# Pairing token tiles for seven block products from the third batch on

## The chip, the cores and the metric

The kernel runs on one core of one Trainium2 chip. The metric is the device time of one launch in microseconds (us). The engines named here are TensorE (PE, matmuls; PEld is its weight load), VectorE (DVE), ScalarE (ACT), GpSimd (POOL) and SyncE (SP), which issues DMAs.

## What is computed

Attention with RMS-normalised q and k (8 batches, 12 heads, 448 positions, head size 64), and behind it a feed-forward layer with a PReLU (768 to 2048 to 768) on the 3584 tokens:

```python
q_n, k_n = rmsnorm(q, g_q), rmsnorm(k, g_k)      # x / sqrt(mean(x*x) + 1e-6) * g
scores = np.matmul(q_n, k_n.transpose(0, 1, 3, 2)) / 8
attn = softmax(scores)                           # over the keys
x = np.matmul(attn, v)                           # heads side by side: (3584, 768)
h = x @ w_in                                     # (3584, 2048)
g = np.maximum(h, 0.0) + alpha * np.minimum(h, 0.0)
out = g @ w_out                                  # (3584, 768), float32
```

## The kernel before

**Groups and steps.** Four heads of a batch make a group y (three per batch, 24 in all). A group's scores are seven tiles of 128 keys by 2x448 queries. Lines 679 to 719 deal these 168 tiles out to 69 steps; the main loop (line 917) issues one step after the other, and since the schedule is manual, the order of the code is the order of every engine's queue. A step has two to four score tiles; some steps also have a softmax denominator (`dens`), a product with v (`avs`), the turn of a group's q and k, and then fillers (`gaps`) that keep TensorE at work. A pair of groups (y, y+1) has its denominator in one step and its product with v in the next (41 and 42, 57 and 58). The third group of a batch, from y = 8 on, has both in one step (28, 36, 44, 52, 60, 68).

**What a group needs.** `load_qk` brings q and k on SP (ring "nat"), `square` squares them on POOL (ring "sq"), `reduce` sums on DVE, `root` makes the inverse root on ACT (two operations on rr, lines 173 and 174), `scale` multiplies on POOL (ring "qs", line 179), `turn_dma` transposes by DMA on SP (rings qT, kT), and `turn` multiplies kT by the gains on DVE (line 288). `soft` (line 343) takes the exponential of a score tile on ACT. For the third group of a batch, `add_up` sums these exponentials over the tiles on POOL, six additions (line 356), and `den_pre` makes the denominator from that sum with matmuls "dnb" (line 389), which DVE copies (line 397); ACT then takes logarithm and exponential (lines 401 and 410), and DVE multiplies the product with v by it into xT (line 439).

**Fillers.** `up(b, ft)` makes one of 16 blocks of g for a batch: six matmuls (line 454), alpha times h on ACT into a tile "ah" (line 494), the maximum on DVE into gT (line 498). `down(b0, t, oh)` makes one half of the columns of one tile of 128 tokens: 16 matmuls (line 508), a copy on DVE (line 520), two DMAs. gT holds two batches, seven token tiles. Lines 773 to 850 deal the fillers out by a cost for each (`UP` 1.13, `DOWN` 2.6).

**Banks.** ups, downs, dnb and half of the products with v take turns on two PSUM banks (`psf`, tag "mm"). The next user of a bank waits until the last reader of it is done.

**Block products.** The last six token tiles (22 to 27) are done in pairs: `quad` computes two tiles times w_out, cut in 2x2 blocks, with seven block products of eight matmuls each in place of eight. It needs sums of blocks of g (`mix`, on POOL, lines 563 to 566) and differences of blocks of w_out (`mix_weights`, 16 operations on POOL at the end of step 60, line 554):

```python
nc.gpsimd.tensor_add(out=g[:, 0], in0=block(t + 1, 0), in1=block(t + 1, 1))
nc.gpsimd.tensor_sub(out=g[:, 1], in0=g[:, 0], in1=block(t, 0))
nc.gpsimd.tensor_sub(out=g[:, 2], in0=block(t, 0), in1=block(t + 1, 0))
nc.gpsimd.tensor_sub(out=g[:, 3], in0=block(t, 1), in1=g[:, 1])
```

After step 68 come one down, the 16 ups of the last batch, and the three quads.

Of the kernel before, what the change touches and what calls it, by code (L numbers as in the profile page):

```python
# [9 lines left out]
FP32 = mybir.dt.float32  # L10
# [11 lines left out]
def kernel(  # L22
# [72 lines left out]

    nat, sqs, qs, ss_t, rr_t, qkT, vt, xT = {}, {}, {}, {}, {}, {}, {}, {}
# [3 lines left out]
    def load_qk(y, hold=False):  # L100
        b, i = divmod(y, G)
        for nm in "qk":
            t = ld.tile([128, 2, J, D], FP32, name="nat", tag="nat", bufs=6)
            if hold and nm == "q":

                nc.scalar.copy(out=t[:, 0, 0, 0:1], in_=expb)
            for g in range(2):
                (nc.scalar if y < 2 and g else nc.sync).dma_start(
                    out=t[ds(64 * g, 64)].rearrange("p h j d -> p h (j d)"),
                    in_=SRC[nm][b, g, :, ds(2 * i, 2)],  # L110
                )
            nat[y, nm] = t

    def load_v(b):
        t = att.tile([128, HH, J, D], FP16, name="vt", tag="vt")
# [28 lines left out]
    def square(y, nm):  # L144
        src = nat[y, nm].rearrange("p h j d -> p (h j d)")
        sq = ld.tile([128, 2 * J, D], FP32, name="sq", tag="sq", bufs=4)
# [29 lines left out]
    def scale(y, nm):  # L176
        t = ld.tile([128, J, 2, D], FP16, name="qs", tag="qs", bufs=4)
# [11 lines left out]
    def part_square(nm, h, j, eng):  # L189
        if ("sq", nm) not in tops:  # L190
            tops["sq", nm] = ld.tile([128, 2 * J, D], FP32, name="sq", tag="sq", bufs=4)
# [24 lines left out]
    def part_scale(nm, j, n, eng):  # L216
        if (0, nm) not in qs:
            qs[0, nm] = ld.tile([128, J, 2, D], FP16, name="qs", tag="qs", bufs=4)
# [15 lines left out]
    def part_copy(nm, j, eng):  # L234
        if (0, nm) not in qkT:
            qkT[0, nm] = att.tile([128, J, 2, 64], FP16, name=f"{nm}T", tag=f"{nm}T", bufs=4)
# [17 lines left out]
    def turn_one(y, nm):  # L254
# [6 lines left out]
        t = att.tile([128, J, 2, 64], FP16, name=f"{nm}T", tag=f"{nm}T", bufs=4)  # L261
# [12 lines left out]
    def turn_dma(y):  # L274
        for nm in "qk":
            t = att.tile([128, J, 2, 64], FP16, name=f"{nm}T", tag=f"{nm}T", bufs=4)
# [7 lines left out]
    def turn(y):  # L284
# [20 lines left out]
        for tp, nm in zip(tps, "qk"):  # L305
            t = att.tile([128, J, 2, 64], FP16, name=f"{nm}T", tag=f"{nm}T", bufs=4)
# [166 lines left out]
    def up(b, ft, spare=False):  # L473
# [8 lines left out]
        ah = ffn.tile([128, S], FP16, name="ah", tag="ah", bufs=3)  # L482
        if b == 0 and ft in (2, 3, NF - 4):

            nc.vector.tensor_scalar(
                out=ah, in0=hT[:, :S], scalar1=alpha_sb[:, ft : ft + 1], scalar2=None,
                op0=ALU.mult,
            )
            if ft < 4:

                held.append((hT, ah, ft))
                return
        else:
            nc.scalar.activation(  # L494
                out=ah, in_=hT[:, :S], func=AF.Copy, scale=alpha_sb[:, ft : ft + 1]
            )
        for hT, ah, ft in [(hT, ah, ft)] + (held if b == 0 and ft == 4 else []):
            nc.vector.tensor_max(out=gT[:, ft, ds((b & 1) * S, S)], in0=hT[:, :S], in1=ah)  # L498

    def down(b0, t, oh, jobs=(), spare=False):  # L500

        op = bank("op", spare)
        parts = 2 if (b0, t, oh) == (B - 2, J - 1, 1) else 1
        PW = OH // parts
        ops = [op] + [bank("op", False) for _ in range(parts - 1)]
        for c in range(parts):
            for ft in range(NF):
                nc.tensor.matmul(  # L508
                    out=ops[c][:, :PW],
                    lhsT=gT[:, ft, ts(t, 128)],  # L510
                    rhs=w_out_sb[:, ft, ds(oh * OH + c * PW, PW)],
                    start=(ft == 0),
                    stop=(ft == NF - 1),
                )
# [3 lines left out]
        o = ffn.tile([128, OH], FP32, name="osb", tag="osb", bufs=4)  # L518
        for c in range(parts):
            nc.vector.tensor_copy(out=o[:, ts(c, PW)], in_=ops[c][:, :PW])  # L520
# [3 lines left out]
        last = (b0, t) == (B - 2, J - 1)  # L524
        for c in range(parts):
            for half in range(2):
                bb, j = divmod(2 * t + half, J)
                (nc.scalar if last and half else nc.sync).dma_start(
                    out=out4[b0 + bb, j, :, ds(oh * OH + c * PW, PW)],
                    in_=o[ds(64 * half, 64), ts(c, PW)],  # L530
                )

    HF = NF // 2
    QF = HF // 2
    tw, mixes = {}, {}

    def mix_weights():

        def w(f, m, p):
            return w_out_sb[:, ds(HF * f + QF * p, QF), ts(m, OH)]  # L540

        for p in range(2):
            for n in range(4):
                tag, bufs = ("nat", 6) if (p, n) not in ((1, 2), (1, 3)) else ("sq", 4)
                tw[n, p] = ld.tile([128, QF, OH], FP16, name="tw", tag=tag, bufs=bufs)
        for n, x, y in (
            (0, (0, 1), (0, 0)), (1, (1, 1), 0), (3, (1, 0), 1), (2, (1, 1), (0, 1))
        ):
            for p in range(2):
                a = w(*x, p)  # L550
                b = tw[y, p] if y in (0, 1) else w(*y, p)
                for c in range(2):
                    r = ts(c, QF // 2)
                    nc.gpsimd.tensor_sub(out=tw[n, p][:, r], in0=a[:, r], in1=b[:, r])

    def block(t, f):
        return gT[:, ts(f, HF), ts(t, 128)]

    def mix(t):

        g = att.tile([128, 4, HF, 128], FP16, name="gs", tag="expT", bufs=EB)
        mixes[t] = g
        nc.gpsimd.tensor_add(out=g[:, 0], in0=block(t + 1, 0), in1=block(t + 1, 1))  # L563
        nc.gpsimd.tensor_sub(out=g[:, 1], in0=g[:, 0], in1=block(t, 0))
        nc.gpsimd.tensor_sub(out=g[:, 2], in0=block(t, 0), in1=block(t + 1, 0))
        nc.gpsimd.tensor_sub(out=g[:, 3], in0=block(t, 1), in1=g[:, 1])

    def send(b0, t, oh, o, c=slice(0, None), split=False):
        for half in range(2):
            bb, j = divmod(2 * t + half, J)  # L570
            dst = out4[b0 + bb, j, :, ts(oh, OH)]
            (nc.scalar if split and half else nc.sync).dma_start(
                out=dst[:, c], in_=o[ds(64 * half, 64), c]
            )

    def quad(b0, t, wide, last=False):

        s1, s2, s3, s4 = (mixes[t][:, n] for n in range(4))
# [15 lines left out]

        def whole(f, m):
            return lambda ft: w_out_sb[:, HF * f + ft, ts(m, OH)]

        def mixed(n):
            return lambda ft: tw[n, ft // QF][:, ft % QF]

        def product(bank, g, v, first, c=slice(0, OH)):
            for ft in range(HF):
                nc.tensor.matmul(  # L603
                    out=bank[:, c], lhsT=g[:, ft], rhs=v(ft)[:, c],
                    start=(first and ft == 0), stop=(ft == HF - 1),
                    skip_group_check=True,
                )

        def part(name):
            return ld.tile([128, OH], FP32, name=name, tag="qs", bufs=4)  # L610

        def result():
            return ffn.tile([128, OH], FP32, name="osb", tag="osb", bufs=4)

        u = {}

        def m1():
            product(x, block(t, 0), whole(0, 0), True)
            u[1] = part("m1")
# [469 lines left out]
```

## Time and profile before

| what | us |
| --- | --- |
| median of 3 runs (423.75 to 424.4) | 424.37 |
| the profiled execution | 425.34 |
| its span, first to last instruction | 423.5 |
| ACT busy | 278.4 (66%) |
| steps 10 to 68 begin | 36.7 to 368.6 |
| ups and quads after step 68 end | 419.6 |

The mean granted TensorE clock is 0.992: it is 0.83 between 10 and 30 us, and 1.00 from 30 us on. A line of a group gives the source line, the engine and operation, what it writes and reads with the shape, the count, busy time and mean ns of one, and the engine's idle time just ahead of it with what ended it. A line of a timeline gives start, duration, engine, line, operation, and in brackets the idle time before it. The steps' starts are the starts of their first score tiles (line 329).

### The profile page before, as it was taken

The page shows a single profiled execution, that of the slowest core. Times are in us where ns is not written, and L with a number is a line of the kernel's source. Part 1 is how long each engine was busy: PE and PEld are TensorE (multiplying, and loading weights), DVE is VectorE, ACT ScalarE, POOL GpSimd, SP SyncE. Part 2 cuts the span into 40 slices and gives each one's busy share as a digit, 9 for nine tenths or more (in the row PEclk, how much of TensorE's full clock was granted, in tenths as well). Part 3 has the DMA queues.
Part 4 walks back from the last instruction along what each step waited for, and adds up shares of the span by engine and source line. Part 5 has one row for each costly group of instructions (what it writes and reads, how often), then busy time and mean ns, then how long its engine had stood idle before and what let it go on. Part 6 is the DMA issues. An engine that isn't in the chain of part 4 may idle for free.

```text
span 423.5 us, 11140 instructions
## 1 busy us (share of the span) xinstructions
PE 411.3 (97%) x4731; PEld 214.7 (51%) x4731; DVE 224.7 (53%) x335; ACT 278.4 (66%) x390; POOL 290.9 (69%) x201
## 2 busy tenths in 40 slices
PE   7899999999999999999999999999999999999996
PEld 3335445544455545554555545554555545555564
DVE  3866964556474545547465364646464253455322
ACT  5798888778856677667847578467865478155110
POOL 6689995384996479481993649753790999960870
PEclk9889999999999999999999999999999999999999
DMA  8999999999756974649255973548215500110144
GB/s 184 239 240 211 193 207 184 201 212 220 129 125 112 195 141 108 104 98 218 58 129 97 174 183 86 98 100 177 46 38 104 107 14 21 29 30 2 29 96 101
DMA packets 68530, 53.37 MB, mean 126 GB/s; under 512 B 35568, under 2 KB 68480, under 8 KB 68480
## 3 DMA queue, kind: packets, MB, share of 16 engines
q1 hardware_dynamic: 53520, 39.54, 43.4%
q0 software_dynamic: 13984, 11.81, 18.8%
q10 hardware_dynamic: 976, 1.31, 1.2%
q8 instruction: 37, 0.61, 0.6%
q14 instruction: 13, 0.11, 0.1%
HBM read 45.62 MB, written 11.01 MB: 134 GB/s over the span
## 4 chain that ended last, share of the span: by engine, by line
PE 85%; ACT 6%; DVE 4%; POOL 2%; DMA 1%; issue 1%; POOLq 0%; ACTq 0%
PE op L508 23%; PE hT L454 21%; PE sc L329 8%; PE hTa L454 8%; PE av L368 5%; PE opa L508 4%; ACT expT L343 3%; PE oq L603 3%; PE dn L368 3%; POOL rden L356 2%; PE avb L368 2%; PE oqm L603 2%; ACT ah L494 2%; PE dnb L389 2%; PE spin L671 1%; DVE gT L498 1%
## 5 line engine op out<-in xcount | busy, mean ns | idle before, releaser
L343 ACT ACTIVATE expT<-sc,expb 128x896 f16<-128x896 f32 x168 | 161.6, 1003 | 44.7 <-PE sc L329 44.4
L179 POOL TENSOR_TENSOR qs<-nat,rr 128x896 f16<-128x896 f32 x41 | 69.1, 1707 | 81.7 <-issue 39.3
L454 PE MATMUL hT<-xT,w_in_sb 128*128 128x448 f16 x558 | 115.7, 353 | 0.8 <-DVE gT L498 0.5
L454 PEld LDWEIGHTS <-w_in_sb 128*128 128x128 f16 x768 | 73.2, 98 | 74.0 <-issue 9.4
L508 PE MATMUL op<-w_out_sb,gT 128*128 128x384 f16 x592 | 101.4, 326 | 0.5 <-DVE gT L498 0.5
L508 PEld LDWEIGHTS <-gT 128*128 128x128 f16 x704 | 66.1, 98 | 53.0 <-issue 11.8
L494 ACT ACTIVATE ah<-hT,cols 128x448 f16<-128x448 f32 x92 | 58.1, 632 | 41.8 <-PE hT L454 40.9
L498 DVE TENSOR_TENSOR gT<-hT,ah 128x448 f16<-128x448 f32 x93 | 57.9, 623 | 48.8 <-ACT ah L494 48.0
L155 POOL TENSOR_TENSOR sq<-nat 128x896 f32<-128x896 f32 (+1 forms) x47 | 75.4, 1625 | 8.4 <-DMA nat<-in_q_dram 7.8
L356 POOL TENSOR_TENSOR rden<-rden,expT 128x896 f32<-128x896 f32 x30 | 56.8, 1895 | 2.4
L329 PE MATMUL sc<-qT,kT 64*32 64x448 f16 (+1 forms) x1092 | 54.9, 359 | 3.5 <-ACT expT L343 1.4
L163 DVE TENSOR_REDUCE ss<-sq 128x14 f32<-128x896 f32 (+1 forms) x48 | 48.8, 1038 | 2.5 <-POOL sq L155 2.5
L520 DVE COPY osb<-op 128x384 f32<-128x384 f32 x37 | 20.5, 556 | 53.0 <-PE op L508 52.5
L454 PE MATMUL hTa<-xT,w_in_sb 128*128 128x448 f16 x198 | 42.8, 352 | 0.0
L329 PEld LDWEIGHTS <-kT 64*32 64x32 f16 (+1 forms) x1092 | 16.6, 93 | 36.1 <-issue 29.8
L494 ACT ACTIVATE ah<-hTa,cols 128x448 f16<-128x448 f32 x33 | 20.9, 634 | 15.3 <-PE hTa L454 15.2
L498 DVE TENSOR_TENSOR gT<-hTa,ah 128x448 f16<-128x448 f32 x33 | 20.6, 624 | 17.6 <-ACT ah L494 17.0
L439 DVE TENSOR_TENSOR xT<-av,rden 128x896 f16<-128x896 f32 x16 | 17.5, 1091 | 21.5 <-ACT rden L410 15.5
L368 PEld LDWEIGHTS <-vt 64*32 64x32 f16 (+1 forms) x1260 | 21.7, 94 | 12.4 <-issue 2.5
L368 PE MATMUL av<-expT,vt 64*32 64x448 f16 (+1 forms) x812 | 26.3, 349 | 0.0
L508 PE MATMUL opa<-w_out_sb,gT 128*128 128x384 f16 x112 | 19.4, 327 | 0.0
L563 POOL TENSOR_TENSOR gs<-gT 128x1024 f16<-128x1024 f16 x3 | 6.4, 2122 | 16.7 <-DVE gT L498 16.7
(98 smaller groups left out, 331.9 us busy)
## 6 DMA issues: line engine op xcount, KB each, us to landing
nat<-in_q_dram SPq DMA_DIRECT2D x46, 224.0 KB, 4.4
nat<-in_k_dram SPq DMA_DIRECT2D x46, 224.0 KB, 4.7
out_dram<-osb SPq DMA_DIRECT2D x107, 96.0 KB, 2.2
vt<-in_v_dram POOLq DMA_DIRECT2D x16, 336.0 KB, 5.8
w_in_sb<-in_moe_w_in_dram POOLq DMA_DIRECT2D x12, 256.0 KB, 7.4
w_out_sb<-in_moe_w_out_dram POOLq DMA_DIRECT2D x4, 768.0 KB, 12.1
nat<-in_q_dram ACTq DMA_DIRECT2D x2, 224.0 KB, 4.6
nat<-in_k_dram ACTq DMA_DIRECT2D x2, 224.0 KB, 5.8
```

What stands on the lines that cost most here:

```text
L155: nc.gpsimd.tensor_mul(out=sqf[:, c], in0=src[:, c], in1=src[:, c])
L163: nc.vector.tensor_reduce(out=o[:, c], in_=sqs[y, nm][:, c], axis=AXIS_X, op=ALU.add)
L179: eng.tensor_mul(out=t.rearrange("p j h d -> p h j d"), in0=nat[y, nm], in1=rr_t[y][:, "qk".index(nm)].unsqueeze(3).broadcast_to((128, 2, ...
L329: nc.tensor.matmul(out=sc[ds(64 * g + m * c, m), par, :S].rearrange("p (j c) -> p j c", j=J), lhsT=kT[ds(64 * par, 64), j, g, ts(c, m)], r ...
L343: nc.scalar.activation(out=expT[y][:, j], in_=scs[y, j][:, :, :S], func=AF.Exp, scale=QK_SCALE, bias=expb[:, 0:1],)
L356: nc.gpsimd.tensor_add(out=s, in0=e[:, 0] if j == 1 else s, in1=e[:, j])
L368: nc.tensor.matmul(out=accs[g][ds(m * h, m), :S], lhsT=weights(g, y, par, ts(c, m), j), rhs=expT[y][ds(64 * g, 64), j, par, :], start=(j = ...
L454: nc.tensor.matmul(out=hT[:, :S], lhsT=w_in_sb[:, g * G + i, ts(ft, 128)], rhs=xT[b][:, g, i, :], start=(i == 0 and g == 0), stop=(i == G ...
L494: nc.scalar.activation(out=ah, in_=hT[:, :S], func=AF.Copy, scale=alpha_sb[:, ft : ft + 1])
L498: nc.vector.tensor_max(out=gT[:, ft, ds((b & 1) * S, S)], in0=hT[:, :S], in1=ah)
L508: nc.tensor.matmul(out=ops[c][:, :PW], lhsT=gT[:, ft, ts(t, 128)], rhs=w_out_sb[:, ft, ds(oh * OH + c * PW, PW)], start=(ft == 0), stop=(f ...
L603: nc.tensor.matmul(out=bank[:, c], lhsT=g[:, ft], rhs=v(ft)[:, c], start=(first and ft == 0), stop=(ft == HF - 1), skip_group_check=True,)
```

## The change

**Pairs from the third batch on.** Tiles 0 to 7 stay downs; tiles 8 to 21 become seven more pairs. A pair's work is cut in three fillers: `quad_a` (three products, 24 matmuls), `quad_b` and `quad_c` (two products each). Each keeps a PSUM bank over two products and adds on DVE. A table written by hand replaces the dealing-out from step 28 on.

```diff
+    def quad_a(tile, jobs=()):
+        s2 = mixes[tile][1]
+        x, y = (psf.tile([128, 512], FP32, name="qx", tag="mm") for _ in range(2))
+        product(x, block(tile, 0), w_block(0, 0), True)
+        u2 = result()
+        nc.vector.tensor_copy(out=u2, in_=x[:, :OH])
+        some(jobs)
+        product(y, s2, tw[1], True)
+        nc.vector.tensor_add(out=u2, in0=y[:, :OH], in1=u2)
+        some(jobs)
+        product(x, block(tile, 1), w_block(1, 0), False)
+        o = result()
+        nc.vector.tensor_copy(out=o, in_=x[:, :OH])
+        send(tile, 0, o)
...
+    def quad_b(tile, jobs=(), late=False):
...
+        product(z, s3, tw[2], True)
+        u3 = result()
+        nc.vector.tensor_add(out=u3, in0=z[:, :OH], in1=u2)
+        some(jobs)
+        product(p, s1, tw[0], True)
+        nc.vector.tensor_add(out=u3, in0=p[:, :OH], in1=u3)
+        send(tile + 1, 1, u3)
...
+    def quad_c(tile, jobs=()):
+        u2, z, p = kept[tile]
+        product(z, block(tile + 1, 1), tw[3], False)
+        o = result()
+        nc.vector.tensor_add(out=o, in0=z[:, :OH], in1=u2)
+        send(tile + 1, 0, o)
+        some(jobs)
+        product(p, mixes[tile][3], w_block(1, 1), False)
+        nc.vector.tensor_add(out=u2, in0=p[:, :OH], in1=u2)
+        send(tile, 1, u2)
...
+    table = (
+        "d d|u4|u4|u4|u4|d d|d|d d|"
+        "a8|b8 c8|u5|u5|u6|a10|b10|c10|"
+        "a12|u4|u4|u4|u4|b12 c12||a14|"
+        "b14 c14|u4|u4|u4|u4|a16|b16|c16|"
+        "a18|u4|u4|u4|u4|b18 c18|a20|b20|"
+    ).split("|")
...
+    rest = list(units("c20 u16"))
```

The table's first entry is step 28, so `a8` is step 36 and `b20` step 67. `some(jobs)` issues one waiting operation, a reduce or a turn of k. Batch 1's ups move a little (steps 21 to 24 get 5, 4, 4 and 3 of them, before 4, 4, 4 and 3), and step 25 gets two downs in place of a down and an up.

**Mixing.** The sums of a pair are made in two parts: s1 and s2 on DVE at the start of a step, s3 and s4 on POOL at the end of one, behind the additions of that step. s3 is written over gT itself. The 16 operations on w_out are spread over steps 17 to 28 and 35, and one of the four differences is written over w_out.

```diff
+    def mix_two(tile, eng, own=False):
...
+        eng.tensor_add(out=s1, in0=block(tile + 1, 0), in1=block(tile + 1, 1))
+        eng.tensor_sub(out=s2, in0=s1, in1=block(tile, 0))
+    def mix_rest(tile):
+        s1, s2, s3, s4 = mixes[tile]
+        nc.gpsimd.tensor_sub(out=s3, in0=block(tile, 0), in1=s3)
+        nc.gpsimd.tensor_sub(out=s4, in0=block(tile, 1), in1=s2)
...
+    for n, y in ((35, 8), (41, 10), (43, 12), (50, 14), (57, 16), (59, 18), (66, 20)):
+        at(n, mix_two, y, nc.vector)
+    for n, y in ((35, 8), (41, 10), (44, 12), (51, 14), (57, 16), (60, 18), (66, 20)):
+        after(n, mix_rest, y)
+    for k in range(3 * PIECES):
+        n, p = divmod(k, PIECES)
+        after(17 + k, mix_weights, (0, 1, 3)[n], p)
+    for p in range(PIECES):
+        after(35, mix_weights, 2, p)
```

**Room.** The mixed blocks stay in SBUF from step 17 on in an "arena" that early loads, squares and scaled tiles borrow first. To make room for it the rings get shorter: nat 6 to 4, sq 4 to 2, qs 4 to 2, qT and kT 4 to 3, v 2 to 1; osb gets 6 in place of 4. The tile ah goes: ACT writes alpha times h into gT and DVE takes the maximum there. From y = 11 on a load is issued behind the scale of the group two before it, and v's load behind the last product of the batch before.

```diff
+        low = y > 3 * G + 1
+        if low:
+            after(root_at[y - 2], load_qk, y)
...
-    for b in range(1, B):
-        at(av_at[G * b] - 6, load_v, b)
+    at(av_at[G] - 6, load_v, 1)
+    for b in range(2, B):
+        after(av_at[G * b - 1] + 1, load_v, b)
```

## The prediction

> **What bounds the kernel now.** I read the page's busy shares first, then the stretches of 10 us, then the groups, and last three timelines step by step.
>
> ```profile
> PE 411.3 (97%) x4731; PEld 214.7 (51%) x4731; DVE 224.7 (53%) x335; ACT 278.4 (66%) x390; POOL 290.9 (69%) x201
> PEclk9889999999999999999999999999999999999999
> L508 PE MATMUL op<-w_out_sb,gT 128*128 128x384 f16 x592 | 101.4, 326 | 0.5 <-DVE gT L498 0.5
> L356 POOL TENSOR_TENSOR rden<-rden,expT 128x896 f32<-128x896 f32 x30 | 56.8, 1895 | 2.4
> ```
>
> TensorE sets the time: 97% busy, and in the stretches from 180 us on it is busy 9.6 to 10 us of every 10. So each matmul removed is time gained, as long as TensorE finds no wait in its place. A mean share hides where that can happen, so I looked at the stage with the least room. POOL, then TensorE, from step 56 to step 60:
>
> ```profile
> 298.56 3.33 POOL L179 TENSOR_TENSOR qs<-nat,rr 128x896 f16<-128x896 f32 x2 [8.50 <-issue]
> 301.86 3.32 POOL L155 TENSOR_TENSOR sq<-nat 128x896 f32<-128x896 f32 x2
> 305.13 1.88 POOL L356 TENSOR_TENSOR rden<-expT 128x896 f32<-128x896 f16 x1
> 307.09 9.80 POOL L356 TENSOR_TENSOR rden<-rden,expT 128x896 f32<-128x896 f32 x5
> ```
>
> ```profile
> 296.33 0.57 PE L329 MATMUL sc<-qT,kT 64*32 64x448 f16 x16
> ...
> 312.00 2.77 PE L508 MATMUL opa<-w_out_sb,gT 128*128 128x384 f16 x16
> 314.71 0.57 PE L329 MATMUL sc<-qT,kT 64*32 64x448 f16 x16
> 315.21 5.37 PE L508 MATMUL op<-w_out_sb,gT 128*128 128x384 f16 x32
> 320.52 0.57 PE L329 MATMUL sc<-qT,kT 64*32 64x448 f16 x16
> 320.90 1.28 PE L389 MATMUL dnb<-rden,ones 64*32 64x448 f32 x12
> ```
>
> Step 56 starts at 296.33. POOL idles until the step's root is there (ScalarE's second rr ends at 298.43), then works without a gap: two scales, two squares, six adds, to 316.89. The denominator matmul dnb, which needs the sixth add, starts at 320.90. **So POOL has 4.0 us of room in this stage, and no more**; it hangs on the start of step 56, so it can't work ahead. In step 28 the room is 0.2 us (adds end 124.38, dnb 124.57). Third, DVE around dnb in step 44:
>
> ```profile
> 220.30 1.91 DVE L288 TENSOR_SCALAR kT<-kT,gain 128x896 f16<-128x896 f16 x1
> ...
> 224.16 1.16 DVE L397 COPY rden<-dnb 128x448 f32<-128x448 f32 x2 [1.18 <-PE dnb L389]
> 227.38 1.09 DVE L439 TENSOR_TENSOR xT<-av,rden 128x896 f16<-128x896 f32 x1 [2.06 <-ACT rden L410]
> 228.39 2.07 DVE L163 TENSOR_REDUCE ss<-sq 128x14 f32<-128x896 f32 x2
> 230.37 1.25 DVE L520 COPY osb<-op 128x384 f32<-128x384 f32 x2
> ```
>
> DVE stands still for 2.06 us for ScalarE's logarithm and exponential; what is queued behind xT waits too. Today that is a copy nobody needs soon.
>
> **What goes.** Seven more pairs (tiles 8 to 21), each of 56 matmuls of 384 columns in place of 64, so 56 matmuls in all. A group of 16 takes 2.60 us between starts (315.21 to 320.52 holds 32 and two score tiles), 162.5 ns each: 56 x 162.5 ns = **9.1 us** less. The last three pairs stay. Moved at no cost: the 16 tw pieces leave the end, and with them most of the wait before dnb in step 68 (368.4 to 369.4, worth 1.0 us). The ah tile goes; ScalarE writes gT itself, after matmuls that the new table finishes steps earlier. Shorter nat, qs, q/k and v rings: each load or turn comes 4 to 7 steps (some 24 us) after the one whose buffer it takes and lands in 3 to 6 us; sends wait on SP behind the same scales as now. I cost these at nothing; were a load late once per batch it would be 1 to 2 us each.
>
> **What comes, by stage.** Natural arrival is what TensorE would reach without new waits. An up unit is 1.14 us, a down 2.6, the thirds of a pair a, b, c 3.9, 2.6, 2.6.
>
> Steps 17 to 28 (T1). Nine tw pieces (1.65 us each, the L554 rows) enter POOL ahead of the sixth add of y 8: 14.9 us. One fits a wait for a load (82.4 to 85.3). The other eight, 13.2 us, have the 5.6 us idle before 106.06 and 1.1 us more because step 24 begins one up later; 6.5 are left. TensorE comes 2.6 us later (a down more, the same ups), less the 1.1 us already counted, and 0.2 was free, so dnb waits **4.8 us**. If only the two pieces behind step 24's scales counted, it would be 3.3 - 1.5 - 0.2 = 1.6.
>
> Steps 40 to 44 (T3). mix_rest adds two POOL operations of 2.12 us (the gs rows) before adds four to six: 4.25. TensorE's own work shrinks from 17.2 to 15.9 (six ups, a, b, c). Room 4.0: 4.25 + 1.3 - 4.0 = 1.5 us. Then the k-turn of step 43 stands on DVE between c's two evictions. Turns took 0.44 us with POOL idle and up to 1.91 (the row above) with POOL busy, ending 0.25 us after POOL's operation. So c's last eviction ends some 0.9 us after the sixth add, and dnb needs that bank: **2.5 us**.
>
> Steps 56 to 60 (T6). The same, with more TensorE work gone: 17.2 to 13.65 (four ups, a, b, c). 4.25 + 3.6 - 4.0 = 3.8, and 0.8 for the turn: **4.6 us**, half at b (it needs s3), half at dnb.
>
> Steps 48 to 52 (T5). No mix before the adds, but step 50 has no filler, a's first bank waits for the xT products, behind the mixing on DVE, and the turn sits between a's evictions: dnb 2.7 us late; c's first product 0.8, its second 0.3: **3.8 us** (0.5 if DVE is free).
>
> Steps 36 and 44 (T2, T4). Quad a follows dnb. Its third product accumulates into the bank that DVE must copy first, and that copy is behind xT (ends 5.76 us after dnb starts; product three could start 5.5 after): 0.85 us. The last copy is behind two reduces of 1.07, and the next unit takes that bank: 1.4 us. **2.2 + 2.25 us.** Step 60 has no reduces (T7): **1.15**.
>
> Steps 66 and 67 (T8). b of tile 20 needs s3, behind three adds: 2.45 us late; less the 1.0 us that goes: **1.45**.
>
> mix_two on DVE (two operations, 1024 f16 columns, both inputs in SBUF) has no row. Below: the turn's 0.44 for 896. Above: 1.23 each, from DVE's L179 of 1.09 for 896, plus up to 1.9 of waiting if POOL is at work. I take 1.23 without the wait, since that row is the nearest with two SBUF inputs. With a wait each time on the path T3, T5 and T6 grow by about 2 us each, +6.
>
> Sum: -9.1 + 4.8 + 2.2 + 2.5 + 2.25 + 3.8 + 4.6 + 1.15 + 1.45 = **+13.65 us**. The profiled execution took 425.34 (span 423.5): 439.0. It stands 1.0 above the median of the runs, 424.37; on that basis 438.0.
>
> One rule speaks on that last doubt. The trace's row: POOL's scale at 30.36 took 2.51 us instead of 1.69, beside DVE's two-input L179 (30.23 to 31.32); the reverse order isn't shown. The Trainium skill, page "SBUF — State Buffer", section "SBUF: two separate sides", says DVE and GpSimd hold a shared port pair as an exclusive lock, also when DVE reads two SBUF inputs. By the page mix_two would wait for POOL's operation each time, and the sum would be about +20.
>
> **Rivals.** (1) Only POOL's sums bind; evictions and banks are hidden: 4.8 + 1.5 + 0.5 + 3.8 + 1.45 - 9.1 = +2.95, 427.3. For it: idle time on DVE is half the span. Against: the order on DVE is fixed. (2) Every mix_two waits for POOL: 13.65 + 6, 444.0. For it: the turn rows. (3) The other side: POOL's chain is not tied to the step, so the scales of steps 24, 40, 48 and 56 start when POOL is free. For it: 8.50 us idle there, which the profile books as "issue". Against: the scales start 0.13 us after rr. If they start 4 us earlier everywhere, dnb finds its adds ready, T1, T3, T5, T6 and T8 fall to about 1.5 together, and 1.5 + 5.6 - 9.1 = -2.0: 422.4; with DVE hidden too, 415.3. It decides once all new waits are under 9.1 us. (4) That fewer matmuls aren't issued can be left out: the loops count them.
>
> **Numbers.** Forecast 0.62 (432 to 443), rival 1 0.18, rival 2 0.07, rival 3 0.11, within 0.2% 0.02 (0.2%, 0.85 us, is what a measurement can tell from no change). Faster 0.11, same 0.02, slower 0.87. The range leaves out rival 3 and the far end of rival 2: 426 to 447.
>
> **What would show it.** TensorE's busy share falls to about 92% (411.3 - 9.1 over 437.2); dnb waits on POOL's rden in steps 28, 44 and 60 and on DVE's evictions; the third product of a waits on DVE after xT in steps 36, 44, 60; b of tiles 16 and 20 wait on POOL's s3. I am wrong if dnb of step 28 waits less than 2 us, if scales start well before their step's rr, or if TensorE stays over 96% busy.

## The result and the profile after

The changed kernel takes **453.69 us** (median of 4 runs, 452.13 to 456.44) against 424.38 (4 runs beside it): a ratio of 1.0695, 95% interval 1.0634 to 1.0756. That is 29.3 us slower. The forecast was 13.65 slower and the range ended at 447.0. The profiled execution took 454.77 us, its span is 453.0 and its mean granted clock 0.970. From here on, lines are those of the changed kernel: score 356, exponential 370, up 481, alpha on ACT 521, maximum 525, down 543, square 178, reduce 186, scale 206, turn of k 315, additions 383, dnb 416, xT 464 and 466, operations on w_out 574, the two sums on VectorE (mix_two) 589 and 590, the two on POOL (mix_rest) 595 and 596, products 600, evictions of a 619 to 626, of b 640 and 643, of c 654 and 658.

The page first, the four rows that were read of before:

```profile
PE 414.4 (91%) x4675; PEld 212.5 (47%) x4675; DVE 268.5 (59%) x370; ACT 278.6 (61%) x390; POOL 323.8 (71%) x215
PEclk9999999996999999989998999899899899999999
L383 POOL TENSOR_TENSOR rden<-rden,expT 128x896 f32<-128x896 f32 x30 | 59.4, 1979 | 3.4 <-ACT expT L370 1.4
L543 PE MATMUL op<-w_out_sb,gT 128*128 128x384 f16 x208 | 35.4, 326 | 0.0
```

TensorE issues 56 matmuls fewer and is yet busy 3 us longer, over a span 29.5 us longer. Busy time that grows while work falls is a slower clock: the PEclk row has a 6 and several 8s from 100 us on, where before had a 9 in every slice from 30 us on. POOL's additions take 1979 ns each, before 1895.

Next the largest waits of TensorE, without those of score tiles for exponentials (3.1 us in nine): line that waited, what released it, us in total, times, longest. Before, no line of this view was over 1.6 us, and the only one behind dnb was 0.2.

```profile
PE hT L481 <- DVE gT L525: 11.4, 6, 6.7
PE dnb L416 <- DVE osb L654: 3.6, 2, 1.8
PE qx L600 <- DVE arena L590: 2.4, 2, 1.4
PE qz L600 <- POOL w_out_sb L574: 2.1, 2, 1.1
PE qx L600 <- DVE xT L464: 1.9, 2, 1.1
```

The largest, 6.7 us, is an ordinary up that waits for an ordinary maximum. Of that pair the change only has the maximum read gT in place of ah, and its time stays (622 ns, before 623); what is new is how long it stands behind other work on VectorE. VectorE, POOL and TensorE of the changed kernel from step 23 on:

```profile
99.34 8.88 DVE L315 TENSOR_SCALAR kT<-kT,gain 128x896 f16<-128x896 f16 x1
108.14 0.61 DVE L525 TENSOR_TENSOR gT<-hT,gT 128x448 f16<-128x448 f32 x1
```

```profile
99.86 1.65 POOL L574 TENSOR_TENSOR arena<-w_out_sb,arena 128x768 f16<-128x768 f16 x1
101.47 3.33 POOL L206 TENSOR_TENSOR qs<-nat,rr 128x896 f16<-128x896 f32 x2
104.76 3.21 POOL L574 TENSOR_TENSOR arena<-w_out_sb,arena 128x768 f16<-128x768 f16 x2
113.38 3.33 POOL L206 TENSOR_TENSOR qs<-nat,rr 128x896 f16<-128x896 f32 x2 [5.41 <-ACT rr L197]
```

```profile
100.81 1.30 PE L481 MATMUL hT<-xT,w_in_sb 128*128 128x448 f16 x6
108.81 2.40 PE L481 MATMUL hT<-xT,w_in_sb 128*128 128x448 f16 x6 [6.70 <-DVE gT L525]
```

The turn of k, 0.44 us with POOL idle and never over 1.91 before, lasts 8.88 us: until 108.22, 0.25 us behind the end of POOL's unbroken run at 107.97 (104.76 + 3.21). The maximum behind it frees a bank that late, and TensorE stands still. And the six matmuls after the wait take 2.40 us in place of 1.30: half the clock. The stretches of 2 us around that wait, with TensorE's busy time (first number behind the comma) and granted clock (third from the end):

```profile
104.00:106.00 2.00, 0.00 (x0) 0.64 0.69 129
106.00:108.00 2.00, 0.00 (x0) 0.50 0.59 115
108.00:110.00 2.00, 1.19 (x4) 0.50 0.85 227
114.00:116.00 2.00, 2.00 (x10) 0.80 0.00 0
```

The clock falls during the wait and comes back only 6 us after work has. Last, the stage of steps 56 to 60, POOL and then TensorE, as it was read before:

```profile
318.70 1.68 POOL L178 TENSOR_TENSOR sq<-nat 128x896 f32<-128x896 f32 x1 [7.19 <-DMA nat<-in_q_dram]
320.64 1.68 POOL L178 TENSOR_TENSOR sq<-nat 128x896 f32<-128x896 f32 x1 [0.25 <-DMA nat<-in_k_dram]
...
333.27 4.22 POOL L383 TENSOR_TENSOR rden<-rden,expT 128x896 f32<-128x896 f32 x2
337.45 2.13 POOL L595 TENSOR_TENSOR gT<-gT 128x1024 f16<-128x1024 f16 x1
339.54 2.12 POOL L596 TENSOR_TENSOR arena<-gT,arena 128x1024 f16<-128x1024 f16 x1
341.62 6.14 POOL L383 TENSOR_TENSOR rden<-rden,expT 128x896 f32<-128x896 f32 x3
```

```profile
322.62 2.04 PE L481 MATMUL hT<-xT,w_in_sb 128*128 128x448 f16 x6 [2.83 <-DVE gT L525]
...
333.80 1.47 PE L600 MATMUL qx<-arena 128*128 128x384 f16 x8 [1.38 <-DVE arena L590]
...
340.66 1.46 PE L600 MATMUL qz<-w_out_sb,gT 128*128 128x384 f16 x8 [0.55 <-DVE xT L464]
...
348.93 1.34 PE L416 MATMUL dnb<-rden,ones 64*32 64x448 f32 x9 [1.80 <-DVE osb L654]
```

Four waits, four causes. A load is late (squares at 318.70 and 320.64, the reduces behind them stand on VectorE ahead of a maximum); a waits for the second sum on VectorE; b waits for xT; dnb waits for c's eviction. dnb of step 44 has the same wait, 1.81 and 0.79 us. What stands ahead of c's evictions there, on VectorE:

```profile
238.85 0.95 DVE L589 TENSOR_TENSOR arena<-gT 128x1024 f16<-128x1024 f16 x1
239.91 2.18 DVE L590 TENSOR_TENSOR arena<-arena,gT 128x1024 f16<-128x1024 f16 x1
242.02 0.54 DVE L654 TENSOR_TENSOR osb<-qz,osb 128x384 f32<-128x384 f32 x1
242.48 1.40 DVE L315 TENSOR_SCALAR kT<-kT,gain 128x896 f16<-128x896 f16 x1
243.80 0.54 DVE L658 TENSOR_TENSOR osb<-qz,osb 128x384 f32<-128x384 f32 x1
```

The second sum takes 2.18 us; alone, in step 66, it takes 0.69. POOL is in the middle of its additions.

**The account.** I add up every pause of over 0.4 us between TensorE's matmuls from 30 us on, counted from start to start less the 0.19 us of a matmul, which gives up to 0.35 us more than the idle time in the brackets of a timeline: before none, after 30.8 us. The slower cadence of ups and products adds 6.9. With the 9.1 us saved that makes 28.6. The profiled executions differ by 29.4 (454.77 less 425.34), though the changed one is 1.8 us ahead at step 16, ahead of all this (its profile has no half clock between 10 and 30 us, that of before a mean of 0.83 there); so 2.6 us aren't in the account, such as pauses under 0.4 us and score matmuls at half clock. So there are two questions: what makes the 30.8, and what the clock has to do with it.

### The profile page after: what moved, and what is told of

Read it like the earlier page. It is cut to its first block, busy times and chain, and to the rows that moved or that the text cites. A ratio compares the mean times of both kernels' runs of the same rounds, so it can differ in the third digit from the quotient of the medians.

```text
span 453.0 us, 11031 instructions
## 1 busy us (share of the span) xinstructions
PE 414.4 (91%) x4675; PEld 212.5 (47%) x4675; DVE 268.5 (59%) x370; ACT 278.6 (61%) x390; POOL 323.8 (71%) x215
## 4 chain that ended last, share of the span: by engine, by line
PE 64%; DVE 11%; POOL 8%; ACT 5%; issue 5%; DMA 4%; SPq 1%; POOLq 0%; DVEq 0%; ACTq 0%
PE hT L481 19%; PE op L543 6%; PE hTa L481 6%; PE qz L600 6%; PE sc L356 5%; PE qx L600 4%; PE av L395 3%; PE oq L600 3%; DMA nat<-in_q_dram 3%; DVE kT L315 3%; ACT expT L370 2%; POOL rden L383 2%; PE dn L395 2%; PE oqm L600 2%; DVE gT L525 2%
## 5 line engine op out<-in xcount | busy, mean ns | idle before, releaser
L525 DVE TENSOR_TENSOR gT<-hT,gT 128x448 f16<-128x448 f32 x95 | 59.0, 622 | 50.8 <-ACT gT L521 50.3
L521 ACT ACTIVATE gT<-hT,cols 128x448 f16<-128x448 f32 x94 | 59.3, 632 | 41.8 <-PE hT L481 41.6
L178 POOL TENSOR_TENSOR sq<-nat 128x896 f32<-128x896 f32 x32 | 54.7, 1726 | 18.1 <-DMA nat<-in_q_dram 10.5
L383 POOL TENSOR_TENSOR rden<-rden,expT 128x896 f32<-128x896 f32 x30 | 59.4, 1979 | 3.4 <-ACT expT L370 1.4
L600 PEld LDWEIGHTS <-gT 128*128 128x128 f16 x320 | 30.6, 99 | 33.6 <-issue 13.7
L186 DVE TENSOR_REDUCE ss<-sq 128x14 f32<-128x896 f32 (+1 forms) x37 | 38.5, 1051 | 5.3 <-POOL sq L178 5.2
L543 PE MATMUL op<-w_out_sb,gT 128*128 128x384 f16 x208 | 35.4, 326 | 0.0
L543 PEld LDWEIGHTS <-gT 128*128 128x128 f16 x256 | 24.0, 98 | 18.5 <-issue 3.6
L525 DVE TENSOR_TENSOR gT<-hTa,gT 128x448 f16<-128x448 f32 x31 | 19.3, 622 | 16.8 <-ACT gT L521 16.5
L315 DVE TENSOR_SCALAR kT<-kT,gain 128x896 f16<-128x896 f16 x17 | 28.2, 1659 | 0.0
L600 PEld LDWEIGHTS <-arena 128*128 128x128 f16 x168 | 17.0, 102 | 15.7 <-DVE arena L590 3.1
L600 PE MATMUL qx<-w_out_sb,gT 128*128 128x384 f16 x112 | 21.5, 338 | 2.8 <-DVE xT L464 1.9
```

The lines of the kernel that those rows point to most:

```text
L178: nc.gpsimd.tensor_mul(out=sqf[:, c], in0=src[:, c], in1=src[:, c])
L315: nc.vector.tensor_scalar(out=t, in0=t, scalar1=gain[:, 0:1], scalar2=None, op0=ALU.mult)
L383: nc.gpsimd.tensor_add(out=s, in0=e[:, 0] if j == 1 else s, in1=e[:, j])
L521: nc.scalar.activation(out=g, in_=hT[:, :S], func=AF.Copy, scale=alpha_sb[:, ft : ft + 1])
L525: nc.vector.tensor_max(out=g, in0=hT[:, :S], in1=g)
L543: nc.tensor.matmul(out=op[:, :OH], lhsT=gT[:, ft, ts(tile % J, 128)], rhs=w_out_sb[:, ft, ts(oh, OH)], start=(ft == 0), stop=(ft == NF - 1),)
```

## The experiments

My theory: POOL's added work holds VectorE off, and what comes late brings half clock. The rivals: the sums and differences are late by themselves (their place in a queue); or the rings, banks and evictions cost, whatever the mixing does. A difference between two kernels is given as the difference of their ratios to the kernel before, times 424.4 us. The changed kernel's own ratio is uncertain by 0.006, 2.6 us, so a difference from it under 3 us decides nothing.

### The turn by itself: POOL work in the kernel before

Six products of a block of w_out with ones, on POOL at the end of step 22 of the kernel before (w_out keeps its values). Once on six blocks, once all on the same block, so that each waits for the one ahead.

```diff
+    def again():
+        for n in range(6):
+            t = w_out_sb[:, n].rearrange("p (a c) -> p a c", c=64)    # or w_out_sb[:, 0]
+            one = ones.unsqueeze(1).broadcast_to((128, 12, 64))
+            nc.gpsimd.tensor_mul(out=t, in0=t, in1=one)
+    after(22, again)
```

> The kernel before with six more operations on POOL at the end of step 22 (w_out blocks times one, each in a block of its own, so that none waits for another; the values stay). Theory A: POOL works without a gap from the squares on until these are done, so the k-turn of step 23, 0.69 us in the kernel before, takes as long as the run, 8 to 10 us; TensorE waits 5 to 7 us behind DVE there, its clock falls, and the time grows by 8 to 13 us. Theory B: the turn stays under 2 us; only POOL's lateness counts, about 10 us of work less 5.6 us of idle time, seen as a wait of dnb in step 28, 4 to 5 us in all.

> The same six operations, all on one block, so that each waits for the one before it. POOL's work is the same within 0.5 us. Theory A: a chain leaves a short gap on POOL between two operations, as between the additions on rden (0.08 us), and the turn slips into the first one: it takes under 2.5 us, TensorE doesn't wait in step 23, and only the lateness at dnb of step 28 is left, +4 to +6 us. Theory B: as m1_run, within 1 us of it.

Independent: 434.24 us, ratio 1.0244 (1.0229 to 1.0259). Chained: 429.94, 1.0137 (1.0111 to 1.0163). VectorE around the turn, and POOL, with independent operations and then with chained ones:

```profile
98.50 10.06 DVE L294 TENSOR_SCALAR kT<-kT,gain 128x896 f16<-128x896 f16 x1
98.72 9.58 POOL L252 TENSOR_TENSOR w_out_sb<-w_out_sb,ones 128x768 f16<-128x768 f16 x6
109.14 2.40 PE L460 MATMUL hT<-xT,w_in_sb 128*128 128x448 f16 x6 [7.87 <-DVE gT L504]
```

```profile
98.13 0.90 DVE L294 TENSOR_SCALAR kT<-kT,gain 128x896 f16<-128x896 f16 x1
97.14 10.25 POOL L252 TENSOR_TENSOR w_out_sb<-w_out_sb,ones 128x768 f16<-128x768 f16 x6
125.87 1.77 PE L395 MATMUL dnb<-rden,ones 64*64 64x448 f32 x8 [3.15 <-POOL rden L362]
```

The same six operations at the same time hold the turn for 10.06 us or for 0.90. Chained operations leave a pause between them (10.25 us for six, against 9.58), and the turn slips in behind the first. So it isn't one POOL operation that holds the turn in the first kernel, but all six. (A pause isn't needed everywhere; see the last section.) With the turn out of the way the six operations cost what the prediction's T1 describes, dnb of step 28 waits 3.15 us for POOL. Both came out as theory A expected; the turn and TensorE's wait of 7.87 us are a little longer than its 8 to 10 and 5 to 7.

### The turn on ScalarE

```diff
-            nc.vector.tensor_scalar(
-                out=t, in0=t, scalar1=gain[:, 0:1], scalar2=None, op0=ALU.mult
-            )
+            nc.scalar.activation(out=t, in_=t, func=AF.Copy, scale=gain[:, 0:1])
```

In the changed kernel, and in the one before as a control:

> The changed kernel, with the k-turn from group 7 on (kT times gain) done by ACT in place of DVE. Theory A (the turn on DVE can't start while POOL works back to back, what is queued behind it on DVE waits too, and TensorE's clock falls after each wait): the 6.9 us wait of step 23 and the 1.5 us of steps 47 and 48 go, the dnb waits of steps 44 and 51 shrink by 1 to 2 us, and with the half clock after step 23 (10.2 us long) the time falls by 12 to 16 us, to 438 to 442. Theory B (POOL's own sum of work is late, and the turn is only where that shows first): the wait moves to dnb of step 28, where the prediction put 4.8 us, and the time falls by at most 4 us, to 450 or more.

> The kernel before, with the same k-turn on ACT. Both theories: no wait of TensorE hangs on the turn there, and ACT has room, so 424.4 within 1 us. If it falls by more, the turn costs the kernel before something too, and e1 has to be compared with this.

446.45 us, ratio 1.0562 (1.0499 to 1.0626), 5.6 us less; control 426.73, 1.0067 (1.0052 to 1.0082), 2.9 us more than before, which I had not expected. The result lies between the theories. The wait of step 23 is gone, and one comes in its place that the changed kernel didn't have:

```profile
131.25 1.77 PE L414 MATMUL dnb<-rden,ones 64*64 64x448 f32 x8 [4.51 <-POOL rden L381]
```

The wait for dnb of step 28 that T1 foretold was there all along, covered by the longer one ahead of it.

### The mixing, taken out part by part

Each of these leaves work out: the products read plain blocks of g, or of w_out, where a sum or a difference should be. Matmuls, evictions and transfers stay. The third leaves out the 16 operations on w_out, the fourth all of the mixing of tiles 8 to 21 and of w_out.

```diff
# without mix_two               s1, s2 = block(tile + 1, 1), block(tile, 0)
# without mix_rest              s3, s4 plain, for tiles under 22
# without the operations        tw = [w_block(0, 1), w_block(1, 1), w_block(0, 1), w_block(1, 0)]
```

> The changed kernel without the two sums s1 and s2 on DVE for the seven new pairs (plain blocks of g stand in for them, so that part of the computation is left out). Theory A (an operation of DVE that reads two tensors from SBUF waits for POOL's running operation, the second of the two always for a whole one): the waits for s2 in steps 41 and 57 (2.6 us), and most of the dnb waits of steps 44 and 60 (5.5 us), where c's evictions stand behind these sums, go, with the half clock of these places 8 to 12 us, to 442 to 446. Theory B (POOL's sum): only the 0.7 us by which each sum holds POOL up goes, 2 to 4 us, to 450 to 452.

> The changed kernel without s3 and s4 on POOL for the seven new pairs (plain blocks of g stand in, that part of the computation is left out). Theory A: POOL's runs get shorter by two operations, the waits of b for s3 go (steps 42, 58, 67: 3.2 us) and some of dnb's, 5 to 8 us, to 446 to 449; the 6.9 us of step 23 stay. Theory B: with 4.25 us less on POOL ahead of each third group's denominator the waits of steps 42, 44, 58, 60 and 67 all go, 12 us and more, to 441 or less.

> The changed kernel without the 16 operations on w_out (products read plain blocks of w_out in their place, so the output is another); the sums of g stay on VectorE and POOL. With them go the wait of step 23 (6.9 us), the three waits of 1.1 to 1.2 us in steps 36 and 37, and the half clock behind both. Theory A (the three parts of the mixing cost about as much each, and apart from each other: without the two sums it was 10.6 us less, without the other two 9.8, without all three 28): 8 to 11 us less, 443 to 446 us, and dnb of step 28 finds its additions ready. Theory B (they cost jointly, the operations on w_out most of it, since the stages behind start late and bind for that): 14 us less or more, under 440. Theory C (as with the operations moved: what is gained early is lost behind): 449 or above.

> The changed kernel without any mixing for the seven new pairs, and without the differences of w_out (plain blocks of g and w_out stand in; that part of the computation is left out, all matmuls, evictions and rings stay). Both theories put the loss into mixing, on POOL or through its port: then 9.1 us of matmuls are gained and only the waits behind xT in steps 36, 44, 52 and 60 (0.7 us each) and the late load of step 56 (3.0 us, and 1.4 us of half clock) are paid: 417 to 421. If it stays above 424, the pairs' own banks and evictions, or the shorter rings, cost more than the matmuls.

| left out | us | ratio (95%) | less by | pauses | slow cadence |
| --- | --- | --- | --- | --- | --- |
| nothing | 453.69 | 1.0695 (1.0634 to 1.0756) | | 30.8 | 6.9 |
| mix_two | 442.75 | 1.0446 (1.0421 to 1.0471) | 10.6 | 24.4 | 5.8 |
| mix_rest | 443.52 | 1.0464 (1.0416 to 1.0511) | 9.8 | 24.7 | 2.8 |
| w_out operations | 439.80 | 1.0374 (1.0357 to 1.0391) | 13.6 | 24.5 | 1.9 |
| all three | 425.60 | 1.004 (1.002 to 1.0061) | 27.8 | 11.3 | 0.7 |

The w_out operations cost most, 13.6 us for some 26 us of POOL's time. The parts add up to 34.0 where all three give 27.8, so some 6 us would need two of the parts at once; but the intervals of these ratios leave that sum uncertain by nearly 6 us too. mix_two came as theory A had it, mix_rest fell between its theories, and the w_out operations came out at the edge of their theory B. Without any mixing I had expected 417 to 421; it took 425.60. The 9.1 us saved are eaten even then, by 11.3 us of pauses. One, of 1.3 us at 168 us, hangs on nothing that the trace shows; another is 3 us long, in step 56:

```profile
300.66 1.30 PE L481 MATMUL hT<-xT,w_in_sb 128*128 128x448 f16 x6 [2.94 <-DVE gT L525]
```

```profile
296.75 1.68 POOL L178 TENSOR_TENSOR sq<-nat 128x896 f32<-128x896 f32 x1 [7.18 <-DMA nat<-in_q_dram]
```

### The loads

The load of q and k of group y + 2, issued right behind the transposes of group y, ahead of the sends in SP's queue; in the changed kernel, and in the one without mixing.

```diff
-            after(root_at[y - 2], load_qk, y)
...
                 turn_dma(y)
+                if 3 * G + 1 < y + 2 < NG:
+                    load_qk(y + 2)
```

> The changed kernel with each late load of q and k issued right behind the turn by DMA of the group two before it, ahead of that step's output DMAs on SP. In the changed kernel the load of group 22 is issued at 310.2, 3.9 us after that turn, lands late, the reduces of step 55 wait for its squares on DVE and TensorE waits 3.0 us in step 56. Theory A and B: with the load 3.9 us earlier this wait and its half clock go, 3 to 5 us, to 449 to 451. Rival: the loads are late because the transfers themselves take longer (5 to 8 us in place of 4.4), and nothing changes, within 1 us of 453.7.

> The changed kernel without any mixing (every product reads a plain block of g and of w_out, so the output is another; the matmuls, evictions and transfers are the same), and the loads of q and k from group 11 on issued right behind the transposes of the group two before, ahead of the sends. Without mixing alone it took 425.60 us, with 3.1 us of TensorE waiting in step 56 for a late load. Theory A (the shorter rings cost by the place of the loads in SP's queue): that wait goes and nothing comes in its place: 422 to 423.5 us. Theory B (the sixth of the loads has to wait for its buffer anyway, and the additions for dnb are then late instead, as they were with the mixing): 425 to 426 us, with over 2 us of waiting in steps 58 to 60.

With the mixing 450.74 us, 1.0629 (1.0578 to 1.068): 2.8 less, too little to be sure of; the wait of step 56 goes, and step 58 waits 3.4 us in its place. Without the mixing **420.51 us**, 0.992 (0.9903 to 0.9937): 5.1 less, more than theory A's 422 to 423.5 had it, and under the kernel before. POOL's squares of that group then come without a wait:

```profile
288.56 3.33 POOL L178 TENSOR_TENSOR sq<-nat 128x896 f32<-128x896 f32 x2
```

So the place of the loads in SP's queue, which came with the shorter rings, costs about 5 us without the mixing (the wait of step 56 is 3 of them), and the seven pairs are worth 3.4 us (0.8% of 424.4) net of their banks and evictions, if the mixing cost nothing.

### The operations on w_out in other places

Twelve of the 16 operations at the ends of other steps (the four of step 35 stay), two layouts; the second also with the earlier loads:

```diff
-        after(17 + k, mix_weights, (0, 1, 3)[n], p)
+    for k, n in enumerate((15, 15, 16, 16, 24, 24, 24, 29, 30, 31, 32, 33)):   # second: 15, 15, 16, 16, 23, 23, 23, 23, 29, 30, 31, 33
+        after(n, mix_weights, (0, 1, 3)[k // PIECES], k % PIECES)
```

> The changed kernel with 12 of the 16 operations on w_out moved: four to the ends of steps 15 and 16, three to the end of step 24, one each to the ends of steps 29 to 33; the four of step 35 stay. The work on every engine is the same. Theory A (what the mixing costs early on is where POOL's operations stand: they close the gaps in POOL's work around 99 us, which keeps the turn on VectorE waiting, and they stand ahead of the additions for dnb of step 28): the turn of step 23 takes under 2 us, TensorE waits under 0.5 us in step 23 and under 1.5 us for dnb in step 28, the stretch of half clock behind it goes; the 6.9 us of waiting and some 4 of clock go: 441 to 445 us. Theory B (it is the amount of POOL's work, and what is moved binds elsewhere): dnb of step 28 or the products of steps 36 and 37 wait 3 us or more longer than now, 450 or above.

> The changed kernel with the operations on w_out moved: four to the ends of steps 15 and 16, four to the end of step 23, where POOL stood idle for 5.4 us in the first try, one each to the ends of steps 29, 30, 31 and 33; the four of step 35 stay. Theory A (their place in the queue costs): the turn of step 23 takes under 2 us, dnb of step 28 waits under 1.5 us, step 29 begins under 3 us later than before (in the changed kernel 10.3), and 5 us or more of that stay to the end: 444 to 448 us. Theory B (POOL's time costs; what is gained up to step 29 is lost by step 38): 450 or above.

> As the run beside it, and the loads of q and k from group 11 on issued ahead of the sends. Theory A: 2 to 5 us under the run beside it (without mixing the loads were worth 5.1 us, with it 2.8), no wait of TensorE over 1 us in step 56. Theory B (with the mixing, POOL and not the load sets the additions of steps 44, 52 and 60): within 1.5 us of the run beside it.

452.36 us, 1.0663 (1.0623 to 1.0703); 453.52, 1.0676 (1.062 to 1.0731); 453.91, 1.0707 (1.0683 to 1.0731). None differs from the changed kernel. In the first the turn of step 23 takes 0.96 us, but the three operations of step 24 ran behind its scales and squares, ahead of the additions, and dnb of step 28 waits 3.5 us. That is what its theory B had: with the turn free, POOL's lateness binds instead, and nothing is gained. The second has them in the 5.4 us in which POOL stood idle. VectorE and POOL:

```profile
99.93 7.31 DVE L315 TENSOR_SCALAR kT<-kT,gain 128x896 f16<-128x896 f16 x1
```

```profile
97.28 3.35 POOL L206 TENSOR_TENSOR qs<-nat,rr 128x896 f16<-128x896 f32 x2
100.58 6.40 POOL L574 TENSOR_TENSOR arena<-w_out_sb,arena 128x768 f16<-128x768 f16 x4
112.39 3.33 POOL L206 TENSOR_TENSOR qs<-nat,rr 128x896 f16<-128x896 f32 x2 [5.41 <-issue]
```

The operations join the scales into one run to 106.98, and the turn ends at 107.24. Here POOL's idle time was what had let VectorE's turn in. In the third another turn, in step 31, takes 6.11 us behind POOL's run there (153.22 to 159.70), and TensorE pauses 4.1. Theory A fell both times; the earlier loads gave nothing on top, as theory B of that run had it.

### All that helped, together

The first has the first layout, the earlier loads, and the squares of groups 17, 20 and 23 on ScalarE. The other two have the second layout with the turns on ScalarE, the last one with the earlier loads too.

> The changed kernel with the operations on w_out moved as in the run beside it, the loads issued ahead of the sends, and the squares of groups 17, 20 and 23 on ScalarE in place of POOL (3.3 us less for POOL ahead of the additions of steps 44, 52 and 60). Theory A (POOL's time in the steps that end in a dnb is what the rest of the loss hangs on): dnb of steps 44, 52 and 60 waits under 1 us each, b of tiles 16 and 20 finds s3 ready, 433 to 439 us. Theory B (ScalarE, which has to wait for the loads with its exponentials queued behind, or VectorE, which still waits for POOL with the two sums and the turns, binds then): 440 to 446 us. Neither expects it under the kernel before, 424.4.

> The changed kernel with the turns of k on ScalarE and the operations on w_out at the ends of steps 15, 16, 23, 29, 30, 31, 33 and 35. Theory A (POOL's idle time is free for POOL's own work, and what it cost was the turn on VectorE): no wait over 1 us in steps 23 to 34, dnb of step 28 waits under 1 us (5.8 us with the turns on ScalarE alone), step 29 begins at most 3 us later than before, and the time is 4 to 7 us under that of the turns on ScalarE alone (446.45): 439.5 to 442.5 us. Theory B (the stages behind give it back, as step 37 did): 445 or above.

> As the run beside it, and the loads of q and k from group 11 on issued ahead of the sends. Theory A (in the run without it that had the earlier loads, a wait of 4.1 us in step 31 came from a turn on VectorE behind POOL, which is gone here): 1.5 to 4 us under the run beside it, no wait over 1 us in step 56. Theory B (ScalarE with the turns behind its exponentials, or POOL ahead of dnb, binds): within 1 us of the run beside it.

451.82 us, 1.067 (1.0635 to 1.0705): no better than the changed kernel and above both theories (433 to 439, 440 to 446), and dnb of steps 28, 44 and 60 wait 3.5, 2.5 and 2.5 us. With the turns off VectorE: 443.64, 1.0467 (1.0445 to 1.0489), 9.7 us less, and 4.0 less than the turns on ScalarE alone. It is just short of theory A's 442.5. POOL's idle time is free now: from step 23 to step 35 no pause is over 0.4 us, and step 29 begins 1.9 us later than before, where the changed kernel had 10.3. The rest, 25 us of pauses, stands from step 36 on. TensorE's waits in that run:

```profile
PE qz L598 <- POOL gT L593: 4.8, 3, 1.7
PE dnb L414 <- DVE osb L652: 4.6, 2, 2.8
PE qz L598 <- POOL w_out_sb L572: 3.8, 4, 1.1
PE qx L598 <- DVE arena L588: 2.8, 2, 1.8
```

All four, 16.0 us together, are the mixing: sums on POOL, evictions behind the two sums, the last four w_out operations, the second sum itself. The earlier loads on top give 442.42, 1.0419 (1.0384 to 1.0453): 2.0 us less by the ratios, where the two intervals leave some 1.7 us open, so hardly clear of the noise. It is the fastest version of the change here that computes the whole, and still 18 us slower than before.

## Why the prediction was wrong

The direction and most places were right; the size was half. By its terms, with the pauses of over 0.4 us at the place of each (they add up to the 30.8):

| term | foretold | pauses | what stood there |
| --- | --- | --- | --- |
| T1, steps 17 to 28 (and 32) | 4.8 | 7.5 | the starved turn in step 23 (6.9), not dnb |
| T2, steps 36 and 37 | 2.2 | 3.4 | third product of a 1.1; w_out operations 2.4 |
| T3, steps 41 to 44 | 2.5 | 5.4 | second sum 1.1, xT 0.7, dnb 3.6 |
| T4, steps 47 and 48 | 2.25 | 1.5 | ups behind the maximum, the first (1.1) behind a turn of 3.09; none at the place named |
| T5, steps 51 and 52 | 3.8 | 3.1 | an exponential 1.1, xT 1.3, c behind b's eviction 0.7 |
| T6, steps 56 to 60 | 4.6 | 7.2 | late load 3.0, second sum 1.5, xT 0.7, dnb 2.0 |
| T7 | 1.15 | 0 | |
| T8, steps 66 and 67 | 1.45 | 2.7 | as named; the 1.0 to go stayed |
| sum | 22.75 | 30.8 | |
| clock | 0 | 6.9 | |

**The gain** of 9.1 stood: the run without mixing and with early loads is 3.4 us under the kernel before with 7.3 us of pauses left.

**T1, failed in its mechanism.** I counted POOL's time against TensorE's arrival at dnb and found 4.8 us. With the turn on ScalarE that wait came, 4.67 us and two of 0.6 behind it. But I took a turn on VectorE as 0.44 to 1.91 us, "ending 0.25 us after POOL's operation", and read it as the end of one operation; so the turn of step 23 had no term. There it is the end of POOL's run. The w_out operations closed the pauses in POOL's work: from 85.51 to 107.97 there is none, and the turn, which comes up at 99.34, waits for the end of it. The 1.91 of before was no bound of the turn; it held for the POOL work that stood beside it then.

**mix_two, wrong in price and in what follows.** I took 1.23 us each "without the wait". Alone it takes 0.68 and 0.69; beside POOL the second takes 2.18 to 2.27, as rival 2 had it (I gave it 0.07). The Trainium skill, page "VectorE: DVE Perf Modes", section "The perf-mode tier table (the rule you actually need)", gives 1224 ns for 2048 elements of 16 bits from SBUF; an estimate from that is some 0.65 to 0.7 us for 1024, and the trace agrees. I had taken the row of a float32 operation as the nearest. What I did not see at all is that c's evictions stand behind the two sums on VectorE and give dnb its banks: the 1.8 us of step 44 stay even with nothing of mix_rest on POOL (1.69 us in that run, behind a second sum of 2.05). Those of step 60 go there: POOL is idle beside the second sum, which takes 0.69.

**"I cost these at nothing" failed.** The shorter rings cost some 5 us without the mixing. My cover was that each load has 24 us; but the load of step 56 stands on SP behind a group's transposes and sends, and its squares come when TensorE is there already. My price if the cover went was 1 to 2 us per batch; it was one wait of 3 in one batch.

**The w_out operations of step 35** have no term. I noted that the moved operations leave the end, and never asked where the last four land: on POOL 190.26 to 196.69, with b of tile 8 reading them piece by piece from 193.32 on.

**The bank of T4 and T7.** I had "the next unit takes that bank". The first up of step 45 started at 253.22 while the third product's bank was still being copied, to 253.91, so it had the other bank. In T4 and T7 dnb took so long that VectorE had caught up before a's third product.

**The clock had no term.** 6.9 us, a quarter of the loss: waits that were priced as their own length brought half clock behind them.

Of the signs that I named, TensorE's share (91%, foretold 92), dnb in steps 44 and 60 (behind c's evictions, not behind POOL's rden) and b of tile 20 came; and the one that I said would show me wrong came too, dnb of step 28 waited under 2 us.

What stays open: how much of the 6.9 us would be left with fewer, shorter waits, since no run here takes it out by itself; and why some turns are let in between two POOL operations and others not. The account leaves 2.6 us.

## What to carry over

An engine's idle time is not free where another engine shares a port with it: ask of each piece that you move into it which operation elsewhere lives on that pause, and price that one at up to the length of the whole run you make. Of a wait, price the clock behind it as well. And ask of each wait what it covers: here the wait for the turn hid the one for dnb, and two other placings of the same operations moved the waits and gave nothing.

## What the runs showed of the hardware

**VectorE's turn can be held over a whole run of POOL's operations.** It took 0.44 us with POOL idle, 0.90 beside six chained POOL operations, 10.06 beside six independent ones, 7.31 and 8.88 beside runs of scales and w_out operations. The Trainium skill, page "SBUF — State Buffer", section "SBUF: two separate sides", has the one that comes second blocked for the whole of the other's instruction. The second sum's 2.18 to 2.27 us agree with that; these turns show more, a block over a run of instructions. But not every run holds it. In the first layout above, another turn comes up in the first of three w_out operations back to back, and ends at 115.32, just behind that first one (113.43 and a third of 4.97 make 115.09):

```profile
114.44 0.88 DVE L315 TENSOR_SCALAR kT<-kT,gain 128x896 f16<-128x896 f16 x1
113.43 4.97 POOL L574 TENSOR_TENSOR arena<-w_out_sb,arena 128x768 f16<-128x768 f16 x3
```

In the changed kernel the turns at 183.19 and 242.48 get in the same way between two squares back to back, in 1.40 us each. So a pause of POOL is not always needed, and what decides is not shown here.

**Half clock behind small waits.** It comes in stretches of 3.4 us and multiples: 10.2 us around the wait of step 23, in the clock records of the trace. The Trainium skill, page "TensorE: Matmul & The Clock Gate", section "What's actually happening", has half clock after an idle window of about 3.4 us. The wait of step 23 agrees. In steps 36 and 37 no pause is over 1.24 us, and the clock falls too. In these three windows, cut where the clock's own records change, TensorE is busy 2.49, 1.32 and 3.40 us (first number behind the comma), and the granted clock (third from the end) is 1.00, 1.00 and, behind the window that was 39% busy, 0.50.

```profile
189.90:193.31 3.41, 2.49 (x28) 1.00 0.00 0
193.31:196.73 3.42, 1.32 (x14) 1.00 0.00 0
196.73:200.14 3.41, 3.40 (x11) 0.50 0.17 34
```

And the pause of 2.94 us in step 56 without mixing left it at 1.00: it lies across two such windows, busy 2.12 of 3.40 us (from 295.60) and 1.74 of 3.40 (from 299.00). So a window that is half empty can be enough, and a pause can fall between two. Cut in the same way, all the traces here together show 44 falls from 30 us on, each behind a window in which TensorE was busy at most 54%; of the windows behind which the clock stayed at 1.00 only two were under 49%.
